# Turning half the heads' probabilities in 32x32 blocks on VectorE and multiplying them in 32-row tiles on TensorE

## The chip, the cores and the metric

One core of a Trainium2 chip runs the whole kernel. The metric is device time in microseconds of one execution. TensorE (PE, with its weight loads as PEld), VectorE (DVE), ScalarE (ACT), GpSimd (POOL) and SyncE (SP, which issues most DMAs) each run their own queue in order.

## The reference

Sixteen heads (batch 2 x 8) of attention over 768 positions of 64 channels, with a mask: a query sees only keys whose 6 sign bits of a random projection are equal. Two layers of matrix products follow.

```python
q_bits = (np.einsum('bhsd,dk->bhsk', q, proj) > 0)      # k_bits alike; bucket = bits as a number
mask = q_bucket[:, :, :, None] == k_bucket[:, :, None, :]
scores = np.where(mask, scale * np.matmul(q, k.transpose(0, 1, 3, 2)), -1e9)
scores = scores - np.max(scores, axis=-1, keepdims=True)
attn = np.exp(scores)
attn = attn / (np.sum(attn, axis=-1, keepdims=True) + 1e-09)
x = np.matmul(attn, v)                                  # to (1536 tokens, 512)
h = np.maximum(np.maximum(x @ w1, x @ w2), x @ w3) @ w_out
h = h @ w_in                                            # 512 to 2048
g = np.where(h >= 1, h, np.where(h <= -1, 0.0, (h + 1) ** 2 / 4))
out = g @ w_out2
```

## The kernel before

**Attention, one tile.** A head has NK = 6 query tiles of 128 rows, so there are 96 tiles n = 6 h + t. A tile takes these steps. `t_qk` (L369) makes the scores of 128 queries against 768 keys with four matmuls into one of two score buffers `s_ps`; the mask is folded in by extra rows of the operands, and the scores carry a minus sign, so that the maximum is a minimum. `t_max` (L385) copies them to an SBUF tile `p` on VectorE and takes the row minimum at the same time. `t_exp` (L394) makes the exponential in place on ScalarE, with its row sums into `sums`. `t_tr` (L405) turns `p` with six TensorE transposes of 128x128, three into each of two PSUM banks (of three: the two `t_ps` and `pj_ps`). `t_out` (L413) copies each bank into `pt`, on ScalarE or VectorE, whichever the planner finds free first.

**Three tiles make a group.** `g_pv` (L422) multiplies a group of 384 queries: six f32 matmuls with V as the stationary operand (128 keys x 64 channels) and `pt` as the moving one, three key blocks summed on rows 0 to 63 of `u_ps` and the other three on rows 64 to 127. `g_copy` (L443) takes the result to SBUF, `g_fold` (L454) brings the two row halves together by DMA, and GpSimd adds them, multiplies by the reciprocal row sums and splits the result into a high and a low part `x_hl` for the matrix products.

**Preparation.** For each head, K and Q come by one DMA, GpSimd scales and splits them in high and low parts, four DMAs move rows, and TensorE projects the bits (`bits_mm`, L351), which VectorE compares (`bits_rows`, L357).

**Order.** Each step is a task with an engine, a cost, a due time, what it comes after, and the buffers it takes and leaves. A planner (`Work.run`, L76) plays the tasks through with these costs when the program is built and writes each engine's queue in the order that comes out. TensorE's order is written out by hand (L696 to L704): transposes of tile n, scores of tile n + 3, and a group's V product after the next group's first tile. Heads follow one another.

**After attention** come the matrix products (`mlp`), in three-term f32 splits. Their weights come in slices: each is loaded, split on ScalarE, VectorE and GpSimd (`w_steps`, L193) and kept in one of WEARLY early buffers, or, once the attention pools are given up, one of WBUFS - WEARLY later ones (L220). The first steps use tokens of batch 0 and slices 0 to 2.

Of the kernel before, what the change touches and what calls it, by code (L numbers as in the profile page):

```python
# [19 lines left out]
NK = S // 128  # L20
CH = 256
# [91 lines left out]
def lsh_attention_moe_kernel(  # L113
# [3 lines left out]
    v: bass.AP,  # L117
    pj: bass.AP,
# [52 lines left out]
    WEARLY, WBUFS = 5, 7  # L171
# [88 lines left out]
    def attention(mlp_steps):  # L260
        with ExitStack() as ax, ExitStack() as sx:
            raw_p = ax.enter_context(tc.tile_pool(name="raw", bufs=2))
            prep_p = ax.enter_context(tc.tile_pool(name="prep", bufs=3))
            v_p = ax.enter_context(tc.tile_pool(name="v", bufs=2))
            p_p = ax.enter_context(tc.tile_pool(name="p", bufs=3))
            pt_p = ax.enter_context(tc.tile_pool(name="pt", bufs=3))
# [3 lines left out]
            t_ps = [ps_s.tile([128, 512], F32, name=f"t_ps{i}") for i in range(2)] + [pj_ps]  # L270
            NH, NT_ = B * H, B * H * NK
            head, pair, tl, grp = {}, {}, {}, {}

            def warm_up(count, i):
                for _ in range(count):
                    nc.tensor.matmul(out=t_ps[i][:, 0:CH], lhsT=warm[:, 0:128], rhs=warm, start=True, stop=True)


            def load_head(h, parts=1):
# [6 lines left out]
                head[h] = dict(r=r)  # L286

            def load_v(h):
                vr = v_p.tile([128, NK, D], F32, tag="vr", name="vr", bufs=3)
                nc.sync.dma_start(out=vr, in_=v[h])  # L290
                head[h]["vr"] = vr
# [72 lines left out]
            def bits_both(h, bank):  # L364
                for half in range(2):
                    bits_mm(h, half, t_ps[bank.at], 64 * half)


            def t_qk(n):  # L369
# [3 lines left out]
                for half in range(2):  # L373
                    ks = slice(half * HALF, (half + 1) * HALF)
                    o = s_ps[n % 2][:, half, 0:HALF]
# [9 lines left out]
            def t_max(n):  # L385
                nm = sm_p.tile([128, 1], F32, tag="nm", name="nm", bufs=4)
                p = p_p.tile([128, S], F32, tag="p", name="p")
                nc.vector.tensor_scalar(  # L388
                    out=p.rearrange("p (a k) -> p a k", a=2), in0=s_ps[n % 2][:, :, 0:HALF], scalar1=MASKED, scalar2=MASKED,
                    op0=ALU.min, op1=ALU.min, accum_out=nm,  # L390
                )
                tl[n] = dict(nm=nm, p=p)

            def t_exp(n):  # L394
                h, t = divmod(n, NK)
                if n % (2 * NK) == 0:
                    pair[h // 2] = dict(sums=nm_p.tile([128, 64], F32, tag="sums", name="sums")[:, 0:2 * NK])
# [4 lines left out]
                    accum_out=pair[h // 2]["sums"][:, c:c + 1],  # L402
                )

            def t_tr(n, half, bank):  # L405
                for j in range(3):
                    kt = 3 * half + j
                    nc.tensor.transpose(  # L408
                        out=t_ps[bank.at][:, j * 128:(j + 1) * 128],
# [3 lines left out]
            def t_out(n, half, bank, copy):  # L413
                g, r = divmod(n, 3)
                if g not in grp:
                    grp[g] = pt_p.tile([128, NK, HALF], F32, tag="pt", name="pt")
                copy(  # L417
                    out=grp[g][:, 3 * half:3 * half + 3, r * 128:(r + 1) * 128],
                    in_=t_ps[bank.at][:, 0:HALF].rearrange("p (j q) -> p j q", j=3),
                )  # L420

# [8 lines left out]

            def block(g, bits, bank):
                if bits:
                    bits_both(bits, bank)
                    for half in range(2):
                        bits_rows(bits, half, t_ps[bank.at], 64 * half)
                    work.at["DVE"] = work.at.get("DVE", 0.0) + 1.38
                g_pv(g, 0, 3)
# [16 lines left out]
            def g_fold(g):  # L454
                pr, cs = g_cut(g)
                if g % 4 == 0:
                    pr["uc"] = nm_p.tile([128, S], F32, tag="uc", name="uc", bufs=1)
# [22 lines left out]
            def pair_rows(p_, bank=pj_ps):  # L480
                nc.tensor.transpose(out=bank[0:2 * NK, 0:128], in_=pair[p_]["sums"], identity=ident)

            def pair_copy(p_, bank=pj_ps):
                rt = nm_p.tile([2 * NK, 128], F32, tag="rt", name="rt", bufs=1)
                nc.scalar.copy(out=rt, in_=bank[0:2 * NK, 0:128])
# [64 lines left out]
            raw_s = {x: Slots(1) for x in ("rb", "rt", "u_ps", "uc")}  # L550
            raw_s["prep"] = Slots(3)
            raw_s["pt"], raw_s["t"] = Slots(3), Slots(3)
            raw_s |= {x: Slots(2) for x in ("r", "uo", "s", "xr", "sums", "u", "d")}
            raw_s["p"] = Slots(3)
            raw_s["vr"] = Slots(3)
# [4 lines left out]
            def task(eng, cost, due, fn, *args, **kw):  # L560
                return work.add(eng, cost, lambda: fn(*args), due, **kw)
# [6 lines left out]
            def head_tasks(h):  # L568
                due = NK * h - 11
# [16 lines left out]
                if h == 1:  # L586
                    bp = place("t", 1)
                    mm = task("PE", 0.66, due + 1, bits_both, h, bp, after=[hi], takes=[bp], leaves=[rp])
                    order["bits"] = [mm]
                    rows = [  # L590
                        task("DVE", 0.69, due + 1, lambda half=half: bits_rows(h, half, t_ps[bp.at], 64 * half), after=[mm])
                        for half in range(2)
# [8 lines left out]
            def v_tasks(h):  # L601
                due = NK * h - 2
                vr = place("vr", 2)
                v_place[h] = vr
                if h > 0:
                    vready[h] = task("SP", 0.35, due, load_v, h, takes=[vr], lag=3.0)
# [4 lines left out]
            sums_p, u_p, uc_p, exps, adds, pt_p_ = {}, {}, {}, {}, {}, {}  # L611

            def tile_tasks(n):
                h, t = divmod(n, NK)
                g, r = divmod(n, 3)
                sp, pp = place("s", 1), place("p", 2)
                tb = [place("t", 1) for i in range(2)]
                if n % (2 * NK) == 0:
# [333 lines left out]
```

## Time and profile before

| | |
|---|---|
| median of 3 runs | 694.81 us (693.83 to 695.39) |
| profiled execution, its own time | 694.73 us |
| its span, first to last instruction | 693.0 us |
| TensorE busy | 683.4 us (99%) |
| VectorE busy | 491.3 us (71%) |
| ScalarE busy | 344.9 us (50%) |
| GpSimd busy | 273.0 us (39%) |

The profiled execution is one run; its time lies close to the median, and 1.7 us of it lie outside the span. A busy time is the union of an engine's instructions. Matmuls are pipelined, so a new one starts before the one ahead is recorded as ended, and a busy TensorE says less than the pace at which its instructions follow one another. In the span three stages can be told apart: the start to 14.80 us, attention to 231.65, and the matrix products.

### The profile page before, as it was taken

Reading aid. Unit: us, or ns where it says so; the run is one execution under the profiler, and the core shown is the slowest. Engines: PE = TensorE matmul, PEld = TensorE weight load, DVE = VectorE, ACT = ScalarE, POOL = GpSimd, SP = SyncE. Lnnn points to the kernel's source line nnn. Section 1 sums busy time; section 2 is a strip of 40 time slices with the busy share of each in tenths; the row PEclk is TensorE's granted clock in tenths of the full one; section 3 lists DMA queues with packets and bytes.
Section 4 is the critical chain, followed back from the end, with each engine's and each line's share of the span. In section 5 each row is a group of like instructions: output and inputs, shape, how many; then the busy total and the mean of one; then the engine's idle time right before and its main releaser. Section 6 shows DMA issues by size and latency. Waiting matters only on the chain.

```text
span 693.0 us, 9878 instructions
## 1 busy us (share of the span) xinstructions
PE 683.4 (99%) x3516; PEld 541.3 (78%) x3516; DVE 491.3 (71%) x758; ACT 344.9 (50%) x669; POOL 273.0 (39%) x248
## 2 busy tenths in 40 slices
PE   7999999999999999999999999999999999999998
PEld 4777777677767688888888888888888888888886
DVE  6778787787776586775444356765888888888844
ACT  3777677777768333332322233665454444554430
POOL 4234564654730334443232112534434434434430
PEclk9999999999999999999999999999999999999999
DMA  5656576475541322221112022121111112211104
GB/s 157 131 135 142 138 195 159 115 177 140 141 101 39 107 92 91 92 92 53 47 45 69 31 70 88 56 78 45 61 61 62 61 61 66 85 62 61 31 0 183
DMA packets 26281, 62.76 MB, mean 91 GB/s; under 512 B 3940, under 2 KB 10692, under 8 KB 26232
## 3 DMA queue, kind: packets, MB, share of 16 engines
q1 hardware_dynamic: 26200, 62.12, 31.6%
q8 instruction: 28, 0.46, 0.3%
q14 instruction: 21, 0.17, 0.1%
q0 software_dynamic: 32, 0.00, 0.0%
HBM read 42.04 MB, written 3.19 MB: 65 GB/s over the span
## 4 chain that ended last, share of the span: by engine, by line
PE 94%; DVE 4%; ACT 1%; issue 1%; DMA 0%; DVEq 0%; ACTq 0%
PE b L746 47%; PE b L873 19%; PE u_ps L426 8%; PE t_ps L408 6%; PE s_ps L378 4%; PE s_ps L381 4%; PE pj_ps L408 3%; DVE p L388 1%; PE t_ps L352 1%; PE pj_ps L352 1%; DVE q L359 1%; DVE pt L417 1%; DVE lo L312 0%; ACT p L400 0%; DMA r<-in_kq 0%
## 5 line engine op out<-in xcount | busy, mean ns | idle before, releaser
L746 PE MATMUL b<-x_hl,w 128*128 128x512 f32 (+1 forms) x900 | 202.0, 381 | 0.0
L746 PEld LDWEIGHTS b<-x_hl,w 128*128 128x128 f32 x900 | 163.9, 188 | 33.1 <-issue 0.6
L773 POOL TENSOR_TENSOR g<-r,g 128x512 fp32r<-128x512 f32 x48 | 62.5, 1303 | 121.3 <-ACT g L772 121.3
L873 PE MATMUL b<-w,g 128*128 128x512 f32 (+1 forms) x438 | 105.9, 386 | 0.0
L388 DVE TENSOR_SCALAR_CACHE_REDUCE p<-s_ps 128x768 f32<-128x768 f32 x96 | 91.6, 956 | 15.8 <-PE s_ps L381 13.8
L400 ACT ACTIVATE p<-p,nm 128x768 f32<-128x768 f32 x96 | 90.1, 939 | 17.9 <-DVE p L388 16.9
L873 PEld LDWEIGHTS b<-w,g 128*128 128x128 f32 x438 | 81.5, 188 | 16.7
L230 POOL TENSOR_TENSOR w<-wg,w 128x512 fp32r<-128x512 f32 (+1 forms) x42 | 59.4, 1414 | 84.4 <-ACT w L224 68.6
L203 DVE SCALAR_TENSOR_TENSOR wg<-wg,wr 128x512 f32<-128x512 f32 (+1 forms) x58 | 66.1, 1140 | 35.6 <-ACT wg L201 34.8
L746 PE MATMUL b<-x_hl,wx 128*128 128x512 f32 x360 | 84.0, 389 | 0.0
L224 ACT CAST w<-wg 128x512 fp32r<-128x512 f32 (+1 forms) x42 | 25.5, 606 | 117.2 <-DVE wg L216 117.2
L746 PEld LDWEIGHTS b<-x_hl,wx 128*128 128x128 f32 x360 | 67.6, 188 | 14.0
L378 PE MATMUL s_ps<-lo,q 128*128 128x384 f32 x192 | 73.2, 381 | 3.5 <-DVE p L388 2.4
L426 PE MATMUL u_ps<-pt,vr 128*64 128x384 f32 x384 | 69.0, 491 | 0.2 <-DVE pt L417 0.2
L381 PE MATMUL s_ps<-hi,q 76*128 76x384 f32 x192 | 65.5, 341 | 0.7 <-DVE hi L343 0.7
L853 DVE SCALAR_TENSOR_TENSOR r<-r,b 128x512 f32<-128x512 f32 x48 | 33.0, 687 | 44.2 <-ACT r L852 44.2
L880 DVE TENSOR_TENSOR acc<-b,acc 128x512 f32<-128x512 f32 (+1 forms) x85 | 56.3, 675 | 7.7 <-PE b L873 7.6
L408 PE MATMUL t_ps<-ident,p 128*128 128x128 f32 x384 | 58.7, 275 | 0.3
L208 DVE TENSOR_SCALAR wg<-wg 128x512 int32<-128x512 int32 (+1 forms) x58 | 53.8, 927 | 2.8
L851 ACT ACTIVATE r<-b,half_sb 128x512 f32<-128x512 f32 x48 | 33.0, 687 | 41.3 <-PE b L746 41.3
L408 PEld LDWEIGHTS t_ps<-ident,p 128*128 128x128 f32 x384 | 45.8, 141 | 9.1 <-issue 4.8
L216 DVE SCALAR_TENSOR_TENSOR wg<-wr,wg 128x512 int32<-128x512 int32 (+1 forms) x58 | 51.7, 892 | 1.0
(87 smaller groups left out, 898.1 us busy)
## 6 DMA issues: line engine op xcount, KB each, us to landing
wr<-in_w SPq DMA_DIRECT2D x48, 512.0 KB
r<-in_kq SPq DMA_DIRECT2D x15, 384.0 KB
q<-hi SPq DMA_DIRECT2D x15, 384.0 KB
vr<-in_v SPq DMA_DIRECT2D x16, 192.0 KB
rb<-d SPq DMA_DIRECT2D x16, 192.0 KB
wr<-in_w SPq DMA_DIRECT2D x8, 384.0 KB
q<-lo SPq DMA_DIRECT2D x15, 192.0 KB
lo<-hi SPq DMA_DIRECT2D x15, 192.0 KB
```

Source lines behind the costliest of these rows:

```text
L203: nc.vector.scalar_tensor_tensor(out=f32(g), in0=f32(g), scalar=TINY_SQ, in1=f32(high), op0=ALU.is_ge, op1=ALU.mult)
L230: nc.gpsimd.tensor_tensor(out=w[:, 1, 0:cols], in0=f32(g2), in1=f32(w[:, 0, 0:cols]), op=ALU.subtract)
L378: nc.tensor.matmul(out=o, lhsT=hd["qa"][:, qs], rhs=hd["lo"][:, ks], start=True, stop=False)
L381: nc.tensor.matmul(out=o, lhsT=hd["qb"][0:76, qs], rhs=hd["hi"][0:76, ks], start=False, stop=True)
L388: nc.vector.tensor_scalar(out=p.rearrange("p (a k) -> p a k", a=2), in0=s_ps[n % 2][:, :, 0:HALF], scalar1=MASKED, scalar2=MASKED, op0=ALU ...
L400: nc.scalar.activation(out=p, in_=p, func=ACTF.Exp, scale=-1.0, bias=tl[n]["nm"], accum_out=pair[h // 2]["sums"][:, c:c + 1],)
L408: nc.tensor.transpose(out=t_ps[bank.at][:, j * 128:(j + 1) * 128], in_=tl[n]["p"][:, kt * 128:(kt + 1) * 128], identity=ident,)
L426: nc.tensor.matmul(out=u_ps[rows, 0:HALF], lhsT=vr[:, kt, :], rhs=grp[g][:, kt, :], start=(i == 0), stop=(i == 2),)
L746: nc.tensor.matmul(out=outp, lhsT=w_[a], rhs=x_[b_], start=(i == 0 and jj == 0), stop=(i == n - 1 and jj == 2),)
L773: nc.gpsimd.tensor_tensor(out=dst[:, 1, cs], in0=src, in1=f32(dst[:, 0, cs]), op=ALU.subtract)
L873: nc.tensor.matmul(out=pb[:, cs], lhsT=gs[f][:, a, tsl], rhs=wt[:, b_, cs], start=(n == 0), stop=(n == len(terms) - 1),)
L880: nc.vector.tensor_tensor(out=acc[:, t, cs], in0=pb[:, cs], in1=acc[:, t, cs], op=ALU.add)
```

## The change

Heads 2, 4, ... 14 (seven heads, 42 tiles) are turned in another way. VectorE transposes the tile `p` in 32x32 blocks into `dt` (`t_turn`), in place of six TensorE transposes and two copies out of PSUM. In `dt` the keys of a block lie on 32 partitions, and which 32 tells which quarter of the 128 queries they belong to. `block4` multiplies a whole head at once: for each of 24 key blocks and each of the four row quarters one matmul of 32 rows x 64 columns, 192 queries wide, the quarters into four banks (`u_ps`, both of `t_ps`, `pj_ps`), even key blocks on rows 0 to 63 and odd ones on 64 to 127. V has to lie on all four row quarters, so it is loaded four times over (`v4`). Three copies (`copy4`) and one DMA (`fold4`) take the result out. The other heads keep their way, but both banks of a tile are copied at once, on ScalarE, while the heads alternate.

The tiles of the turned heads alternate with those of the odd heads (`SEQ`), behind head 0 and the first four tiles of head 1. TensorE's order is written out as strings of steps by place in that sequence: q scores, t transposes, v and w the first and the second part of a V product, b bits, r row sums. `SHIFT` moves the due times of the kinds of tasks. The early weight buffers go from five to three, the prepared heads from three to four, `p` from three to four, `pt` from three to two, `vr` from three to one beside one `v4`. One small constant is loaded by ScalarE's queue, and the scratch for GpSimd's DMAs is smaller.

```diff
-    WEARLY, WBUFS = 5, 7
+    WEARLY, WBUFS = 3, 7
...
-            t_ps = [ps_s.tile([128, 512], F32, name=f"t_ps{i}") for i in range(2)] + [pj_ps]
+            dt = pt_p.tile([128, NK + 2, NB, 32], F32, name="dt", bufs=1)
+            t_ps = ps_s.tile([128, 2, 512], F32, name="t_ps")
...
+            TURNED = range(2, B * H, 2)
+            LEAD = 4
+            first, second = range(NK), [NK * h + t for h in range(1, B * H, 2) for t in range(NK)]
+            DT_AT = {h: 2 * (h // 2 % 2) for h in TURNED}
+            TILES = lambda h: [(t - DT_AT[h]) % NK for t in range(NK)]
+            turned = [NK * h + t for h in TURNED for t in TILES(h)]
+            SEQ = [*first, *second[:LEAD], *(n for ab in zip(turned, second[LEAD:]) for n in ab), *second[LEAD + len(turned):]]
+            SLOT = {n: m for m, n in enumerate(SEQ)}
...
+            def load_v4(h, i):
+                if i == 0:
+                    head.setdefault(h, {})["vr"] = v_p.tile([128, NB, D], F32, tag="v4", name="v4", bufs=1)
+                ks = slice(i * NB // 3, (i + 1) * NB // 3)
+                nc.sync.dma_start(out=head[h]["vr"][:, ks], in_=v4[h, :, ks])
...
+            def t_turn(n):
+                h, t = divmod(n, NK)
+                nc.vector.transpose(out=dt[:, DT_AT[h] + t], in_=tl[n]["p"].rearrange("p (b k) -> p b k", k=32))
+
+            def quarter(q):
+                return (u_ps, t_ps[:, 0], t_ps[:, 1], pj_ps)[q]
+
+            def block4(h, lo, hi):
+                vr, at = head[h]["vr"], slice(DT_AT[h], DT_AT[h] + NK)
+                for kb in range(lo, hi):
+                    cols = UP if kb % 2 == 0 else DOWN
+                    for q in range(4):
+                        rows = slice(32 * q, 32 * q + 32)
+                        nc.tensor.matmul(
+                            out=quarter(q)[cols, 0:NK * 32].rearrange("p (t k) -> p t k", t=NK), lhsT=vr[rows, kb, :], rhs=dt[rows, at, kb],
+                            start=kb < 2, stop=kb >= NB - 2,
+                        )
+
+            def copy4(h, q, count, copy):
+                pr = pair[h // 2]
+                if "u" not in pr:
+                    pr["u"] = nm_p.tile([128, S], F32, tag="u", name="u")
+                to = pr["u"].rearrange("p (t g k) -> p g t k", t=NK, g=4)
+                if count == 1:
+                    copy(out=to[:, q], in_=quarter(q)[:, 0:NK * 32].rearrange("p (t k) -> p t k", t=NK))
+                else:
+                    copy(out=to[:, q:q + 2], in_=t_ps[:, :, 0:NK * 32].rearrange("p a (t k) -> p a t k", t=NK))
+
+            def fold4(h):
+                pr = pair[h // 2]
+                pr["uc"] = nm_p.tile([128, S], F32, tag="uc", name="uc", bufs=2)
+                nc.sync.dma_start(out=pr["uc"][UP], in_=pr["u"][DOWN])
...
+            T_AT, P_AT = 2, 1
+            START = {h: min(SLOT[NK * h + t] for t in range(NK)) for h in range(NH)}
+            raw_s = {x: Slots(1) for x in ("rb", "rt", "u_ps", "t", "b", "v4", "vr")}
+            raw_s |= {x: Slots(2) for x in ("r", "uo", "s", "xr", "sums", "u", "uc", "d", "pt")}
+            raw_s["prep"], raw_s["p"], raw_s["dt"] = Slots(4), Slots(4), Slots(8)
+
+            SHIFT = {prep_hi_scaled: 6.0, t_exp: 42.5, t_out: 2.0, g_copy: 17.5, copy4: -82.0, pair_copy: -20.5, w_tick: 60.0, prep_lo_scaled: -3.0, bits_rows: 4.5, t_max: -12.5, t_turn: 8.0, pair_recip: 20.0}
...
+                    pt_p_[n] = place("dt", 1)
+                    tu = task("DVE", 0.96, m - 1, t_turn, n, after=[ex] + outs.get(h, [])[-1:], takes=[pt_p_[n]], leaves=[pp])
+                    outs.setdefault(h, []).append(tu)
+                    return
...
+                    cp = task(*ways[0][:2], m - 4, t_out, n, hs, ways[0][2], after=[tr], takes=[pt_p_[g]] if r == 0 and (half == 0 or not alone) else [], leaves=[tb])
+                    if alone:
+                        work.also(*ways[1][:2], lambda a=(n, hs, ways[1][2]): t_out(*a), cp)
+                    outs.setdefault(("g", g), []).append(cp)
...
+            def turned_tasks(h):
+                m = max(SLOT[NK * h + t] for t in range(NK))
+                banks = [place("u_ps", 1), place("t", 1), place("b", 1)]
+                blk = None
+                for i in range(2):
+                    blk = task(
+                        "PE", 1.955, m + T_AT + 0.5, block4, h, 12 * i, 12 * i + 12, after=[blk] if i else outs[h] + [vready[h]],
+                        takes=[] if i else banks, leaves=[pt_p_[n] for n in turned if n // NK == h] + [v_place[h]] if i else [],
+                    )
+                    order[f"pv{2 * h}.{i}"] = [blk]
+                takes = own(u_p, "u", h // 2, 2)
+                cps = []
+                for q, count, place_, act, dve in ((1, 2, banks[1], 0.5, 0.56), (0, 1, banks[0], 0.35, 0.36), (3, 1, banks[2], 0.35, 0.36)):
+                    cps.append(task("ACT", act, m - 2, copy4, h, q, count, nc.scalar.copy, after=[blk] + cps[:1], takes=[] if cps else takes, leaves=[place_]))
+                adds[2 * h] = adds[2 * h + 1] = task("SP", 0.5, m + 4, fold4, h, after=cps, takes=own(uc_p, "uc", h // 2, 2), lag=4.5)
...
+            first_part = (
+                "q0 q1 B q2 t0 q3 q4 t1 t2 q5 b5 t3 v2 w2 t4 q6 q11 b8 t5 q7 q8 t6 v5 w5 q9 t7 q10 q12 t8 "
+                "q13 q14 t9 v8 q15 t11 q18 w8 q23 q16 t13 b13 q17 t15 v13 w13 q19 r13 t17 q20 b19 q21 t19 "
+            )
+            period = (
+                "q22 q24 v19 w19 t21 q25 q26 v20 w20 q27 t23 q30 q28 t25 b25 q29 q35 t27 v25 w25 q31 r25 "
+                "t29 q32 b31 q33 t31 "
+            )
+            last_part = (
+                "q82 q84 v79 w79 t81 q85 q86 v80 w80 q87 t83 q90 q88 t85 q94 q89 t87 v85 w85 q91 t94 q95 "
+                "r85 t89 q92 q93 t91 t95 v91 w91 t93 v92 w92 "
+            )
+            steps = first_part.split()
...
-        nc.gpsimd.dma_start(out=pc_sb, in_=pc)
+        nc.scalar.dma_start(out=pc_sb, in_=pc)
...
+    v4 = np.tile(v.reshape(B * H, NB, 32, D).transpose(0, 2, 1, 3), (1, 4, 1, 1))
```

## Rows read from the trace of the kernel before

**Rows 1.** The page, engines: busy us (share of the span) x instructions.

```profile
PE 683.4 (99%) x3516; PEld 541.3 (78%) x3516; DVE 491.3 (71%) x758; ACT 344.9 (50%) x669; POOL 273.0 (39%) x248
```

**Rows 2.** Busy times by stage: stretch, length, each engine's busy time, clock, DMA share, GB/s.

```profile
14.80:231.65 216.85, 214.01 (x1400) 153.97 (x1401) 163.78 (x326) 157.14 (x345) 98.79 (x110) 1.00 0.55 134
231.65:254.70 23.05, 23.05 (x137) 20.30 (x136) 17.01 (x27) 7.94 (x15) 6.27 (x5) 1.00 0.33 109
```

**Rows 3.** Chain of waits, 100 to 112 us: start, time on the chain, what.

```profile
102.72 2.09 PE u_ps L426 x12
104.81 0.48 PE pj_ps L408 x3
...
105.61 0.18 PE s_ps L378
...
107.70 0.66 PE t_ps L408 x6
...
109.07 0.80 PE pj_ps L352 x4
109.87 1.94 PE u_ps L426 x12
```

**Rows 4.** Chain of waits over the attention stage, two of its longest pieces.

```profile
22.62 2.09 PE u_ps L426 x12
...
49.28 2.09 PE u_ps L426 x12
```

**Rows 5.** Groups by line and shape, attention stage: count, busy us, mean ns, idle before.

```profile
L388 DVE TENSOR_SCALAR_CACHE_REDUCE p<-s_ps 128x768 f32<-128x768 f32 x95 | 90.6, 956 | 15.8 <-PE s_ps L381 13.8 <-PE t_ps L408 0.6 <-ACT p L400 0.6
...
L400 ACT ACTIVATE p<-p,nm 128x768 f32<-128x768 f32 x96 | 90.1, 939 | 17.9 <-DVE p L388 16.9
...
L426 PE MATMUL u_ps<-pt,vr 128*64 128x384 f32 x384 | 69.0, 491 | 0.2 <-DVE pt L417 0.2
...
L417 ACT COPY pt<-t_ps 128x384 f32<-128x384 f32 x71 | 33.0, 478 | 12.8 <-PE t_ps L408 12.7
...
L417 DVE COPY pt<-t_ps 128x384 f32<-128x384 f32 x57 | 31.3, 553 | 19.8 <-PE t_ps L408 16.0 <-ACT uo L451 1.8 <-ACT u L448 1.6
...
L417 ACT COPY pt<-pj_ps 128x384 f32<-128x384 f32 x39 | 18.7, 479 | 6.1 <-PE pj_ps L408 6.0
...
L417 DVE COPY pt<-pj_ps 128x384 f32<-128x384 f32 x25 | 13.8, 552 | 3.7 <-PE pj_ps L408 3.6
```

**Rows 6.** Timeline of TensorE: f32 projections of one half, and of both halves.

```profile
5.44 0.86 PE L352 MATMUL pj_ps<-r,pj_sc 128*64 128x384 f32 x2
...
109.00 0.87 PE L352 MATMUL pj_ps<-r,pj_raw 128*64 128x384 f32 x4
```

**Rows 7.** Timeline of TensorE's weight loads at the start of a V block.

```profile
102.65 0.20 PEld L426 LDWEIGHTS u_ps<-pt,vr 128*64 128x64 f32 x4 [0.26 <-issue]
...
103.03 0.14 PEld L426 LDWEIGHTS u_ps<-pt,vr 128*64 128x64 f32 x2 [0.18 <-issue]
```

**Rows 8.** Timeline of VectorE in the preparation of head 0.

```profile
6.64 0.36 DVE L343 CAST q<-lo 64x384 fp32r<-64x384 f32 x1
```

**Rows 9.** The page's costliest groups: the weight split on VectorE.

```profile
L203 DVE SCALAR_TENSOR_TENSOR wg<-wg,wr 128x512 f32<-128x512 f32 (+1 forms) x58 | 66.1, 1140 | 35.6 <-ACT wg L201 34.8
```

**Rows 10.** Timeline of VectorE, two minima back to back.

```profile
16.18 0.96 DVE L388 TENSOR_SCALAR_CACHE_REDUCE p<-s_ps 128x768 f32<-128x768 f32 x1
...
17.06 0.95 DVE L388 TENSOR_SCALAR_CACHE_REDUCE p<-s_ps 128x768 f32<-128x768 f32 x1
```

**Rows 11.** What TensorE waited for in the attention stage: total, times, longest.

```profile
PE s_ps L378 <- DVE p L388: 2.4, 3, 1.4
```

**Rows 12.** DMA queues, attention stage: packets, MB, share of 16 engines.

```profile
q1 hardware_dynamic: 14950, 28.73, 54.1%
```

**Rows 13.** Timeline of GpSimd behind the attention stage: weight slices 3 and 4.

```profile
244.86 1.36 POOL L230 TENSOR_TENSOR w<-wg,w 128x512 fp32r<-128x512 f32 x1 [4.33 <-ACT w L224]
...
251.73 1.74 POOL L230 TENSOR_TENSOR w<-wg,w 128x512 fp32r<-128x512 f32 x1
```

More of the change, by code (lines that the diff above doesn't have):

```diff
@@ L586, in head_tasks @@
                 if h == 1:
-                    bp = place("t", 1)
-                    mm = task("PE", 0.66, due + 1, bits_both, h, bp, after=[hi], takes=[bp], leaves=[rp])
+                    bp = place("b", 1)
+                    mm = task("PE", 0.644, due + 1, bits_both, h, after=[hi], takes=[bp], leaves=[rp])
                     order["bits"] = [mm]
                     rows = [
-                        task("DVE", 0.69, due + 1, lambda half=half: bits_rows(h, half, t_ps[bp.at], 64 * half), after=[mm])
-                        for half in range(2)
+                        task("DVE", 0.69, due + 1, bits_rows, h, half, pj_ps, 64 * half, after=[mm]) for half in range(2)
                     ]
@@ L615, in tile_tasks @@
                 g, r = divmod(n, 3)
-                sp, pp = place("s", 1), place("p", 2)
-                tb = [place("t", 1) for i in range(2)]
-                if n % (2 * NK) == 0:
-                    sums_p[h // 2] = place("sums", 1)
+                turned = h in TURNED
+                sp, pp = place("s", 1), place("p", 1 if turned else 2)
+                takes = own(sums_p, "sums", h // 2, 1)
+                qk = task("PE", 0.72, m, t_qk, n, sp, after=ready[h], takes=[sp], leaves=[h_place[h]])
@@ L628, in tile_tasks @@
+                tb = place("t", 2 if alone else 1)
+                tr = None
                 for half in range(2):
[L629 removed]
+                    tr = task("PE", 0.288, m - 4, t_tr, n, half, after=[ex, tr], takes=[] if half else [tb], leaves=[pp], lag=0.1)
                     order[f"tr{n}"] = order.get(f"tr{n}", []) + [tr]
[L631 removed]
@@ L696, in attention @@
-            names = ["qk0", "qk1", "bits", "qk2"]
-            for g in range(NT_ // 3):
-                for n in range(3 * g, 3 * g + 3):
-                    names += [f"tr{n}", f"qk{n + 3}"]
-                    if n == 3 * g and g:
-                        names += [f"pv{g - 1}"] + ([f"rows{g // 4 - 1}"] if g % 4 == 2 else [])
-            line = [t for x in names for t in order.get(x, ())]
-            for a, b_ in zip(line, line[1:]):
-                b_["after"].append(a)
-            low = exps[30]
+            starts = sorted(range(1, NH), key=START.get)
@@ new lines, in attention @@
+            blocks = sorted((g for g in range(NT_ // 3 - 1) if g // 2 not in TURNED), key=lambda g: SLOT[3 * g + 2])
+            BITS = dict(zip(blocks[1:], starts[1:]))
+            assert len(BITS) == len(starts) - 1
+            made = 0
+            for m, n in enumerate(SEQ):
+                h, t = divmod(n, NK)
+                if m == 0:
+                    v_tasks(0)
+                while made < len(starts) and (made < 3 or START[starts[made]] <= m + 18):
+                    head_tasks(starts[made])
+                    v_tasks(starts[made])
+                    made += 1
+                tile_tasks(n)
+                if h in TURNED:
+                    if TILES(h)[-1] == t:
+                        turned_tasks(h)
+                elif n % 3 == 2:
+                    if n < NT_ - 1:
+                        group_tasks(n // 3)
```

218 lines of the change are left out of this document (117 added, 101 removed).

## The prediction

> **What bounds the kernel now.** I read the page's engine shares first, then the busy times by stage, then the chain of waits inside the attention stage, then the groups of instructions of that stage. TensorE is busy for 99% of the span [rows 1], so the question is which of its work goes away and whether it stays fed. The change touches the attention stage alone, 14.80 to 231.65 us, 216.85 us long; TensorE is busy in 214.01 us of it at a granted clock of 1.00, VectorE in 163.78 (76%) and ScalarE in 157.14 (72%) [rows 2]. Busy times of pipelined matmuls overstate their cost, so I take paces from the chain [rows 3]. It runs through TensorE without a gap: a score matmul takes 0.18 us, so the four of a tile some 0.71, its six transposes 0.66, a group of three tiles times V 1.94 to 2.09, the bit projections of a head 0.80. Transposes right after a V block take 0.48 for three where the others take 0.33, so a change of tile shape costs about 0.15. Two heads take 26.66 us (22.62 to 49.28, the same place in the pattern four groups later) [rows 4].
>
> **What is removed on TensorE.** Seven heads of six tiles are turned: 42 x 6 = 252 transposes at 0.66 / 6 = 0.11 us [rows 3], 27.7 us.
>
> **What replaces the multiplication.** Now a head is two groups of six f32 matmuls of 384 columns; the trace holds 384 records for 32 x 6 matmuls, so each is two records [rows 5]. The pair on output rows 0 to 63 and 64 to 127 runs side by side: one f32 matmul of 384 columns alone (two records) spans 0.86 us, two on the two column halves (four records) 0.87 [rows 6]. Three pairs take 1.94 us, 0.647 a pair [rows 3]; a head costs 3.88. After, a head is 24 key blocks x 4 row quarters = 96 matmuls of 192 columns, 192 records and as many weight loads. No row shows a 32-row matmul, so this is the disputed price. From below: if all eight tiles (four row quarters, two column halves) run together, a round of eight takes half of 0.647, and 12 rounds take 3.88, no change. From above: if only the column halves run together, 48 pairs x 0.323 = 15.5 us, 11.6 more per head and 81 more in all. Between them lies the issue: the first four loads of a V block are over after 0.20 us where two take 0.14 [rows 7], so two more cost 0.06, 0.03 each with no overlap; if loads and matmuls together were issued no faster, 384 x 0.03 = 11.5 us a head. I take the lower end, since the nearest row, two tiles of one array, shows that tiles overlap fully, loads included, and keep the upper ones as rivals.
>
> [...]
>
> The block also takes all of u_ps, t_ps (both banks) and pj_ps at once, so TensorE starts it only when each has been copied out, and the transposes behind it wait for the block's first copy. In the written order two score steps (2 x 0.71) stand ahead of each block and one (0.71) behind, against a copy of 0.48 and a hand-over. If ScalarE has just begun an exponential the copy is late by up to its 0.939 [rows 5]; seven heads, 6.6 us at most. Fewer changes of shape give back 0.15 per head, 1 us, which I leave in that margin.
>
> **VectorE.** It loses its copies of transposed tiles, 82 x 0.553 = 45.3 us [rows 5], and keeps perhaps 12 of them, 6.6, for the ten tiles ahead of the alternation and the two after it. It gains 42 block transposes of 128x768. No row shows one. From below: an f32 copy between SBUF tiles of 64x384 took 0.36 [rows 8], twice that is 0.72. From above: the two-input operation on 128x512 took a mean of 1.14 [rows 9], which at 768 columns is 1.71. I take 0.956, the row of the same size and type (the running minimum), so 40.2 us. Sum: 163.8 - 45.3 + 6.6 + 40.2 = 165.3 us. Back to back the minimum starts every 0.88 us (16.18, 17.06), less than its 0.956 and its accumulator read [rows 10], so there is more room than the sum says.
>
> **ScalarE.** It loses 110 copies x 0.478 = 52.6 us [rows 5] and gets 42 copies of both halves, at most two of 0.478 each, 40.2, and 12 single ones, 5.7. Per turned head three copies replace two, at most 0.48 more, 3.4. Sum 157.1 - 52.6 + 49.3 = 153.8 us. The projections, minima, exponentials, sums and the preparation on GpSimd are the same in number.
>
> **TensorE's sum.** 216.85 - 27.7 = 189.1 us. VectorE would be busy in 87% of that, ScalarE in 81%, so TensorE stays the bound, but with less slack: there are two score buffers and four tiles p. Its waits on VectorE's minima are now 2.4 us in three places [rows 11]. After, VectorE has to be done with a minimum before the score step two later. Between the blocks the written order has stretches such as q27 t23 q30 q28 t25 b25 q29 q35 t27, five score steps in 5 x 0.71 + 3 x 0.66 + 0.80 = 6.3 us; five minima alone take 4.4 of it, so turns of 0.956 are left for the blocks of 3.9 us, in which no score is made. I allow 6 us for the added waits, about one late copy or minimum of an exponential's length in each of the seven alternating stretches; bounds 0 and 14 (two of them).
>
> **DMA.** A turned head's V comes four times over: 768 KB in three pieces for 192 KB, 7 x 576 KB = 4.1 MB more on 28.73 MB, now 54.1% of the engines' time in the stage [rows 12]. In a stage of 195 us that is 54.1 x 32.9 / 28.7 x 217 / 195 = 69%. SP issues three loads and one fold for one load and two folds, one more per head. With one buffer, V of the next turned head is fetched after the block before, and has the rest of the pattern, 26.7 - 4.0 (six tiles' transposes) - 3.9 = 18.8 us; 768 KB at 28.73 MB in 217 us (132 GB/s) take 6 us. I cost it at nothing under that cover; if it went, each late load would stop TensorE by what it is late, 6 us at most. Ready K and Q for the alternating pair come by the same queue; one more prep buffer covers that. The constant moved from GpSimd's queue to ScalarE's, the added buffer of uc, the sums' own place and the smaller scratch are not on the chain: nothing.
>
> **Weights of the next stage.** Three early buffers for five: slice 3 was finished on GpSimd at 246.2 and slice 4 at 253.5 [rows 13], inside the 23.05 us in which TensorE works on slices 0 to 2, to 254.70 [rows 2]. Now slice 3 begins behind the sixth early step, half-way, at 231.65 + 11.5 = 243.2; at the 7.3 us that lie between two slices there [rows 13] it is ready by 250.5, 4 us early, and each next one 7.3 us later for 7.7 us of use. Nothing; without that cover, TensorE waits as long as it is late.
>
> **Sum.** The profiled execution took 694.73 us for a span of 693.0, as the median does (694.81): 694.7 - 27.7 + 6 = 673.0.
>
> **Rivals.** (1) *The tiles overlap in part.* Against: the column pair loses nothing [rows 6]. For: six times as many instructions per multiply, loads of 0.03 and more. A block of 5 to 6 us is 1.2 to 2.1 more for each head, 8 to 15 us: 681 to 688. [...]
> (2) *VectorE becomes the bound.* A turn at 1.71 makes it 165.3 + 42 x 0.75 = 197 busy against 189; counted at the minimum's pace of 0.88 it is some 15 less, 182. Then little slack is left and waits eat 12 to 18 us instead of 6: 679 to 685. Against: a stage at equal loads still drops the copies.
> (3) *The block is bound by issue or runs row by row, and the time is longer.* Place: the 384 instructions of a block. TensorE has 21.7 us to lose, 3.1 per head, so it turns when a block takes over 7.0 us, 18 ns an instruction. At 0.03 it is 11.5: 673 + 7 x 7.6 = 726; row by row 754. For: the loads' spacing [rows 7]. Against: that spacing was seen where the array itself was occupied.
>
> **How the numbers follow.** Forecast 0.60 (667 to 681), rival 1 0.14, rival 2 0.09, rival 3 0.17. Of rival 3, 0.03 comes out within 0.2% (1.4 us, what a measurement here can tell from no change) and 0.14 slower. Faster is 0.60 + 0.14 + 0.09 = 0.83. The range takes in the forecast and rivals 1 and 2 and stops where rival 3 begins, 664 to 694; its low end is 667 less the 1 us of shape changes and 2 of today's waits. What it leaves out is rival 3's slower part and a few hundredths below.
>
> **What would show it.** The attention stage ends at 208 to 213 instead of 231.65; 324 transposes remain; a block of 192 matmul records spans 3.9 us; the turn's mean is near 0.96; TensorE idles under 10 us in the stage; the rest, from the first MLP matmul, is unchanged at 461 us. The prediction is wrong if a block takes over 5 us, if the turn takes over 1.3, or if waits on s_ps or t_ps come to more than 14 us.

## The result, and the profile after

The changed kernel takes 675.67 us (median of 4 runs, 675.43 to 676.23) against 694.44 us (693.83 to 695.39) in the same comparison: a ratio of 0.973, with a 95% interval of 0.9713 to 0.9747. That is 18.8 us less. The forecast was 673.0, with 664 to 694 as its range. The profiled execution took 676.23 us for a span of 674.4.

The page, engines (busy us, share, instructions), to be held against [rows 1]:

```profile
PE 662.3 (98%) x4440; PEld 530.3 (79%) x4440; DVE 492.3 (73%) x725; ACT 337.3 (50%) x625; POOL 273.4 (41%) x247
```

Busy times by stage, with the columns of [rows 2]. The first MLP matmul now starts at 213.06:

```profile
14.80:213.06 198.26, 190.60 (x2312) 140.95 (x2310) 161.87 (x292) 147.22 (x297) 101.24 (x111) 1.00 0.65 166
213.06:236.10 23.04, 23.04 (x136) 20.14 (x135) 14.91 (x24) 6.85 (x13) 3.87 (x3) 1.00 0.30 94
```

The whole gain lies in the attention stage: it ends 18.6 us earlier (231.65 to 213.06), and from there to the end of the span pass 461.3 us, as before (693.0 less 231.65). The granted clock stays at 1.00. TensorE idles for 7.7 us of the stage (198.26 less 190.60), where it was 2.8.

Groups of the stage by line and shape, as in [rows 5] (count, busy us, mean ns, idle before):

```profile
L405 DVE TENSOR_SCALAR_CACHE_REDUCE p<-s_ps 128x768 f32<-128x768 f32 x94 | 87.8, 950 | 11.2 <-PE s_ps L398 8.8 <-PE t_ps L428 0.7 <-issue 0.3
...
L445 DVE STREAM_TRANSPOSE dt<-p 128x768 f32<-128x768 f32 x42 | 40.2, 969 | 9.7 <-PE pj_ps L456 9.3
...
L438 ACT COPY pt<-t_ps 128x768 f32<-128x768 f32 x42 | 33.4, 796 | 12.4 <-PE t_ps L428 12.2
L456 PE MATMUL t_ps<-dt,v 32*64 32x192 f32 x672 | 30.5, 324 | 1.1 <-issue 0.7 <-ACT pt L438 0.4
```

The minimum takes what it took, 0.950 us, and the turn 0.969, 40.2 in all. The copy of both banks takes 0.796, less than two single ones of 0.478 [rows 5]. The next rows are TensorE's timeline at the start of the block of head 4:

```profile
85.43 0.37 PE L456 MATMUL u_ps<-dt,v 32*64 32x192 f32 x1
85.44 0.38 PE L456 MATMUL t_ps<-dt,v 32*64 32x192 f32 x2
85.45 0.37 PE L456 MATMUL pj_ps<-dt,v 32*64 32x192 f32 x1
85.46 0.37 PE L456 MATMUL u_ps<-dt,v 32*64 32x192 f32 x1
85.47 0.38 PE L456 MATMUL t_ps<-dt,v 32*64 32x192 f32 x2
85.48 0.37 PE L456 MATMUL pj_ps<-dt,v 32*64 32x192 f32 x1
85.65 0.32 PE L456 MATMUL u_ps<-dt,v 32*64 32x192 f32 x1
...
85.81 0.32 PE L456 MATMUL u_ps<-dt,v 32*64 32x192 f32 x1
```

Eight records, one for each row quarter and column half, start within 0.05 us, and the next eight 0.16 to 0.22 us later. In the steady part such a round takes 0.162 us, and the 24 rounds of a block 3.9 us. A matmul is two records (192 for the 96 of a block), so eight whole matmuls take two rounds, 0.324 us. That is half of the 0.647 us that a pair of matmuls took before [rows 3], with half as many columns: eight tiles side by side cost no more than two. No loss is to be seen.

The chain of waits for one period of the alternation, from block to block, as in [rows 3, 4] (start, time on the chain, what):

```profile
61.28 0.30 PE u_ps L456
...
64.38 0.31 issue
...
66.20 0.37 PE s_ps L395
...
69.87 0.80 PE pj_ps L369 x4
70.67 0.37 PE s_ps L395
...
72.94 2.08 PE u_ps L480 x12
75.02 0.37 PE s_ps L395
...
77.41 0.80 PE pj_ps L369 x4
78.20 0.37 PE s_ps L395
...
81.19 2.09 PE u_ps L480 x12
83.27 0.81 PE t_ps L428 x6
...
85.50 0.30 PE u_ps L456
...
89.59 0.37 PE s_ps L395
```

Two heads take 24.22 us here, and 23.9 as a mean of the six periods from 61.21 to 204.62, where they took 26.66 [rows 4] and 22.7 (26.66 less 3.96) would have been all of the transposes' gain. Three things are to be seen. A block takes 4.09 us from 85.50 to 89.59, but 4.92 from 61.28 to 66.20, with a hole at 64.38 that the trace puts down to "issue". Behind each of the four narrow steps (32 rows or 64 columns) that a score follows, the first score matmul takes 0.37 instead of 0.18; behind the V product at 81.19, the transposes take 0.81 instead of 0.66. And there are five such visits to narrow shapes in two heads, where there were four: the bits used to stand right ahead of a V product.

What TensorE waited for (total, times, longest), as in [rows 11]:

```profile
PE s_ps L395 <- DVE p L405: 2.7, 2, 1.8
PE t_ps L428 <- ACT pt L438: 2.0, 3, 0.9
...
PE u_ps L480 <- ACT u L467: 0.9, 1, 0.9
...
PE t_ps L456 <- ACT pt L438: 0.4, 1, 0.4
PE s_ps L398 <- DMA hi<-q: 0.3, 1, 0.3
```

Of these waits only 1.4 us fall into the six periods from 61.2 to 204.6 (1.1 for copies, 0.3 for the DMA); the rest lie ahead of them or behind. The DMA queue of [rows 12] now moves this in the stage:

```profile
q1 hardware_dynamic: 16239, 32.61, 63.8%
```

### The profile page after: what moved, and what is told of

Read it like the earlier page. It is cut to its first block, busy times and chain, and to the rows that moved or that the text cites. A ratio compares the mean times of both kernels' runs of the same rounds, so it can differ in the third digit from the quotient of the medians.

```text
span 674.4 us, 11567 instructions
## 1 busy us (share of the span) xinstructions
PE 662.3 (98%) x4440; PEld 530.3 (79%) x4440; DVE 492.3 (73%) x725; ACT 337.3 (50%) x625; POOL 273.4 (41%) x247
## 4 chain that ended last, share of the span: by engine, by line
PE 94%; DVE 2%; DMA 2%; ACT 1%; issue 1%; SPq 0%; DVEq 0%; ACTq 0%
PE b L867 49%; PE b L994 19%; PE s_ps L395 5%; PE u_ps L480 5%; PE t_ps L428 5%; PE s_ps L398 4%; PE u_ps L456 3%; PE pj_ps L369 2%; PE t_ps L456 1%; DVE p L405 1%; DVE lo L329 1%; DMA r<-in_kq 1%; DMA rb<-d 0%; ACT pt L438 0%; PE pj_ps L456 0%
## 5 line engine op out<-in xcount | busy, mean ns | idle before, releaser
L867 PE MATMUL b<-x_hl,wx 128*128 128x512 f32 x684 | 159.6, 389 | 0.0
L867 PEld LDWEIGHTS b<-x_hl,wx 128*128 128x128 f32 x684 | 128.4, 188 | 26.7
L867 PE MATMUL b<-x_hl,w 128*128 128x512 f32 (+1 forms) x576 | 126.8, 376 | 0.0
L867 PEld LDWEIGHTS b<-x_hl,w 128*128 128x128 f32 x576 | 103.1, 188 | 20.7 <-issue 0.6
L420 ACT ACTIVATE p<-p,nm 128x768 f32<-128x768 f32 x96 | 89.7, 935 | 12.3 <-DVE p L405 11.6
L232 POOL TENSOR_TENSOR wx<-wg,wx 128x512 fp32r<-128x512 f32 (+1 forms) x32 | 45.6, 1425 | 65.4 <-ACT wx L226 48.5
L994 PE MATMUL b<-wx,g 128*128 128x512 f32 x288 | 72.1, 389 | 0.0
L994 PE MATMUL b<-w,g 128*128 128x512 f32 (+1 forms) x294 | 71.3, 385 | 0.0
L994 PEld LDWEIGHTS b<-w,g 128*128 128x128 f32 x294 | 54.5, 188 | 11.1
L994 PEld LDWEIGHTS b<-wx,g 128*128 128x128 f32 x288 | 54.0, 188 | 11.2
L232 POOL TENSOR_TENSOR w<-wg,w 128x512 fp32r<-128x512 f32 (+1 forms) x26 | 36.0, 1384 | 58.3 <-ACT w L226 48.1
```

What stands on the lines that cost most here:

```text
L232: nc.gpsimd.tensor_tensor(out=w[:, 1, 0:cols], in0=f32(g2), in1=f32(w[:, 0, 0:cols]), op=ALU.subtract)
L420: nc.scalar.activation(out=p, in_=p, func=ACTF.Exp, scale=-1.0, bias=tl[n]["nm"], accum_out=sums_of(h // 2)[:, c:c + 1],)
L867: nc.tensor.matmul(out=outp, lhsT=w_[a], rhs=x_[b_], start=(i == 0 and jj == 0), stop=(i == n - 1 and jj == 2),)
L994: nc.tensor.matmul(out=pb[:, cs], lhsT=gs[f][:, a, tsl], rhs=wt[:, b_, cs], start=(n == 0), stop=(n == len(terms) - 1),)
```

## The experiments

Each run is set against the changed kernel's 675.67 us; a ratio is to the kernel before on the same chip.

**Rows in turn.** Is the side by side of the row quarters what makes the block cheap?

```diff
-                for kb in range(lo, hi):
-                    cols = UP if kb % 2 == 0 else DOWN
-                    for q in range(4):
+                for q in range(4):
+                    for kb in range(lo, hi):
+                        cols = UP if kb % 2 == 0 else DOWN
```

> The 48 matmuls of each half of a turned head's block are issued quarter by quarter instead of in turn over the four row quarters; the work is the same. If the block is cheap because eight 32x64 tiles run together, only the two column halves are left side by side: 48 pairs x 0.323 = 15.5 us a block for 3.9, seven heads, 81 us more: about 757 us. If the order doesn't matter (tiles wait for each other anyway, or start out of order), about 676.

It took 782.12 us in one run, more than either theory gave. Busy times of three stretches of this run, the first two around the first block, the third over all seven:

```profile
60.00:69.78 9.78, 9.78 (x162) 8.50 (x163) 2.90 (x7) 2.61 (x6) 7.46 (x9) 1.00 0.38 83
69.79:80.02 10.23, 10.23 (x58) 8.77 (x54) 3.57 (x6) 3.62 (x8) 0.00 (x0) 0.50 0.32 90
...
60.00:320.00 260.00, 258.69 (x2057) 197.06 (x2057) 122.37 (x221) 114.43 (x228) 81.44 (x91) 0.76 0.37 96
```

The first block begins at 60.26. Its first half takes 5.76 us at a granted clock of 1.00, which makes an estimated 11.5 us for a block instead of 3.9, so the order decides the price. At 69.79, still inside this block, the granted clock falls from 1.00 to 0.50, though TensorE had been busy for all of the 9.78 us before; the block takes 13.6 us in all. Over the seven blocks the granted clock is 0.76 on average, and the later ones take 18 to 20 us. Of the 106 us more, an estimated 7 x (11.5 - 3.9) = 53 are the order's own; the rest, by difference, goes with the clock.

**Two rows.** The same, with two quarters at a time.

```diff
-                for kb in range(lo, hi):
+                for q0, kb, q in ((q0, kb, q) for q0 in (0, 2) for kb in range(lo, hi) for q in (q0, q0 + 1)):
```

> The matmuls of each half block are issued for two row quarters first and then for the other two: four tiles run together instead of eight. [...]

It took 687.97 us in one run, 12.3 more. A block takes 6.1 us (first round at 86.17, last at 92.16). TensorE's timeline, one round of four records and the start of the next:

```profile
86.39 0.32 PE L456 MATMUL u_ps<-dt,v 32*64 32x192 f32 x1
86.39 0.32 PE L456 MATMUL t_ps<-dt,v 32*64 32x192 f32 x1
86.40 0.32 PE L456 MATMUL u_ps<-dt,v 32*64 32x192 f32 x1
86.41 0.32 PE L456 MATMUL t_ps<-dt,v 32*64 32x192 f32 x1
86.55 0.32 PE L456 MATMUL u_ps<-dt,v 32*64 32x192 f32 x1
```

A round costs the same 0.16 (86.39 to 86.55) with half the tiles in it, which would make 7.8 us a block and 27 us more for seven. Only 6.1 are seen. That the runs of the two pairs of quarters overlap at their ends would fit, as it would for the quarters of the run above (an estimated 11.5 for 15.5), but these rows do not show a place where they meet. From its start to the next step each of the first six blocks takes 6.24 us, 2.15 more than the 4.09 of an undisturbed block of the changed kernel. For seven that makes 15 us; but none of them has a hole like the one at 64.38, and the changed kernel's three holes add 2.8. The clock stays at 1.00. So the side by side of the quarters is shown, with its price: an estimated 11.5 us for one at a time, 6.1 for two, 3.9 for four.

**Short turn, double turn.** How far is VectorE from being the bound?

```diff
-                nc.vector.transpose(out=dt[:, DT_AT[h] + t], in_=tl[n]["p"].rearrange("p (b k) -> p b k", k=32))
+                nc.vector.transpose(out=dt[:, DT_AT[h] + t, 0:1], in_=tl[n]["p"].rearrange("p (b k) -> p b k", k=32)[:, 0:1])
...
-                            out=quarter(q)[cols, 0:NK * 32].rearrange("p (t k) -> p t k", t=NK), lhsT=vr[rows, kb, :], rhs=dt[rows, at, kb],
+                            out=quarter(q)[cols, 0:NK * 32].rearrange("p (t k) -> p t k", t=NK), lhsT=vr[rows, kb, :], rhs=dt[rows, at, 0],
```

> Each turn on VectorE takes 32 of the 768 columns, and the block reads that one key block 24 times; the other key blocks are left out of the result. The queues' order is the same. VectorE loses 42 x (0.969 - some 0.2) = 32 us. If TensorE's own work sets the end, only waits on VectorE go: 1 to 4 us less, 672 to 675. If VectorE is as much the bound as TensorE, 10 us or more less, under 666.

It took 675.87 us, 0.9724 (0.9699 to 0.9748): nothing, although a turn takes 0.203 us instead of 0.969 and VectorE is busy for 28 us less in the span (463.9 for 492.3). Even the 1 to 4 us of the first expectation did not come.

```diff
+                for _ in range(2):
                     nc.vector.transpose(out=dt[:, DT_AT[h] + t], in_=tl[n]["p"].rearrange("p (b k) -> p b k", k=32))
```

> Each turn is made twice, 42 x 0.97 = 41 us more on VectorE, which is busy for 162 of the 198 us of the stage. If TensorE sets the end and VectorE has slack, the slack of some 36 us takes most of it, but in bursts: 5 to 15 us more, 681 to 691. If VectorE is the bound, nearly all of it: 35 to 41 us more, 711 to 717.

It took 703.36 us, 1.0126 (1.0098 to 1.0154): 27.7 of the 41 us added come through, which lies between the two expectations. The granted clock was 0.98 in the stage, which is an estimated 4 us at most (2% of TensorE's 199 busy), so 13 to 17 us were slack. What TensorE waited for then:

```profile
PE s_ps L395 <- DVE p L405: 19.2, 22, 2.1
```

Together: VectorE's work is wholly hidden as it stands, and some 13 us more of it would be.

**Fewer transposes.** Is TensorE still the bound, to the full price of what it loses?

```diff
-                for j in range(3):
+                for j in range(1 if NK + LEAD <= SLOT[n] < NT_ - 2 else 3):
```

> The tiles of the odd heads that alternate with the turned ones make two of their six TensorE transposes; what the others would have written is left out, so the products of those heads are wrong in two thirds of the keys. TensorE loses 42 x 4 x 0.11 = 18.5 us, no other engine loses anything. If TensorE sets the end: 12 to 18 us less, 658 to 664. If VectorE or ScalarE are as much the bound: under 5 less, over 671.

It took 666.48 us, 0.9602 (0.9573 to 0.9631): 9.2 of 18.5 us, again between the two expectations. A step of two transposes takes 0.22 us as expected, but waits come up that were not there:

```profile
PE s_ps L395 <- DVE p L405: 5.0, 14, 0.9
```

**Both less.** Is it VectorE that keeps the other half? Both edits at once.

> The edits of short_turn and fewer_transposes together: 32 of 768 columns turned, two of six transposes made for the odd heads' alternating tiles; the rest of both is left out of the result. Alone they gave 0 and 9 us of the 32 and 18.5 us that they take off VectorE and TensorE. If VectorE's load is what kept the missing transposes from giving more, both together give 14 to 18 us: 658 to 662. If it is the order, ScalarE or the transfers, it stays at 665 to 668.

It took 664.41 us, 0.9574 (0.9558 to 0.959), 2 us below the one edit alone, with intervals that overlap. So VectorE holds back little of the rest or nothing. TensorE's waits are spread, in a profiled execution that took 669.29 us with a granted clock of 0.96 in the stage:

```profile
PE s_ps L398 <- DMA hi<-q: 2.7, 2, 2.3
PE s_ps L395 <- DVE p L405: 2.6, 2, 1.7
```

What else keeps the other 7 us is open.

**Bits at V, early bits.** Fewer visits to narrow shapes: the bit projections right ahead of a V product, as before the change, instead of between score steps; first moved later, then earlier. The repeated part of the order stands here for the others, first the later ones:

```diff
-                "q22 q24 v19 w19 t21 q25 q26 v20 w20 q27 t23 q30 q28 t25 b25 q29 q35 t27 v25 w25 q31 r25 "
-                "t29 q32 b31 q33 t31 "
+                "q22 q24 b19 v19 w19 t21 q25 q26 v20 w20 q27 t23 q30 q28 t25 q29 q35 t27 b25 v25 w25 q31 r25 "
+                "t29 q32 q33 t31 "
```

> In TensorE's written order each bit projection stands directly ahead of a group's V product, as in the kernel before, instead of between score steps. Both have 64-column tiles, so two changes of tile shape at some 0.15 us go for each of 13 projections: 2 to 4 us less than with the change alone, 671.5 to 674. If the projections then come too late for the heads that need them, TensorE waits for their rows: 676 or more.

It took 683.92 us, 0.9848 (0.9819 to 0.9876), 8 more: the expectation missed, the rival held. What TensorE waited for:

```profile
PE s_ps L395 <- DVE p L405: 4.6, 7, 1.5
PE s_ps L398 <- DMA hi<-q: 3.5, 5, 1.1
```

```diff
-                "q22 q24 v19 w19 t21 q25 q26 v20 w20 q27 t23 q30 q28 t25 b25 q29 q35 t27 v25 w25 q31 r25 "
-                "t29 q32 b31 q33 t31 "
+                "q22 q24 v19 w19 t21 q25 q26 v20 w20 q27 t23 q30 q28 t25 b25 q29 q35 t27 b31 v25 w25 q31 r25 "
+                "t29 q32 q33 t31 "
```

> Six of the bit projections are put directly ahead of the V product that comes before their old place, some 4 us earlier: six visits to 64-column tiles fewer, and the rows that the next head waits for come earlier, not later. By the visits' price of 0.25: 1.5 us less, 673.5 to 675. If the projected head isn't split yet at that time, TensorE waits for GpSimd: 676 or more.

It took 681.83 us, 0.982 (0.9803 to 0.9837), 6 more: missed again. Here the data are early, not late, and waits come all the same:

```profile
PE s_ps L395 <- DVE p L405: 3.1, 8, 0.9
PE u_ps L480 <- ACT pt L438: 2.3, 5, 0.5
```

In both, score steps that had a projection between them follow each other directly, and TensorE then waits for minima in seven or eight places instead of two. That a projection there is partly paid for by a wait that it fills fits this. The rows shown account for 5.1 of the 8 us (4.6 + 3.5 less the 3.0 of the profile after) and 2.7 of the 6; the rest was not isolated. The planner also writes the other engines' queues anew for each order.

**Split visits.** The price of a visit itself: the two parts of 15 V products parted by a score or transpose step, same work, 15 visits more.

```diff
-                "q22 q24 v19 w19 t21 q25 q26 v20 w20 q27 t23 q30 q28 t25 b25 q29 q35 t27 v25 w25 q31 r25 "
+                "q22 q24 v19 t21 w19 q25 q26 v20 w20 q27 t23 q30 q28 t25 b25 q29 q35 t27 v25 q31 w25 r25 "
```

> In TensorE's written order one score or transpose step is put between the two parts of 15 V products, so TensorE goes to 64-column tiles and back 15 times more; work and waits for data are the same. If it is such visits that gave back a part of the gain (scores right behind one take 0.90 us for 0.72, and a start 0.1 more than a step elsewhere), 15 x 0.25 = 3.8 us more than the change alone: 678.5 to 680.5. If the longer scores behind them were waits for VectorE or ScalarE, the visits cost nothing by themselves: 675 to 677.

It took 679.21 us, 0.9785 (0.9771 to 0.9798): 3.5 more, 0.24 a visit, as expected. In its chain of waits, one V product in two visits (0.80 and 1.44 for 2.08):

```profile
73.49 0.80 PE u_ps L480 x4
74.28 0.38 PE s_ps L395
...
75.19 1.44 PE u_ps L480 x8
```

The 0.24 is a net figure. Two such places, each from the start of the V product to a later step that stands alike in both orders, take 0.26 and 0.33 us longer than in the changed kernel, an estimated 4.4 us for 15. But the holes inside the blocks, to which the next run turns, add only 1.1 us in this run's profile and 2.8 in the changed kernel's.

**Shifted code.** The holes inside blocks stand in heads 2, 6 and 10 and not in 4, 8 and 12. Is it the place of the tiles in `dt`, which alternates the same way, or the place of the code? 64 small matmuls, 128 instructions, are added ahead of one early tile.

```diff
+                    if n == SEQ[16] and half == 0:
+                        for _ in range(64):
+                            nc.tensor.matmul(out=o[:, 0:32], lhsT=warm[:, 0:128], rhs=warm[:, 0:32], start=True, stop=True)
```

> 64 small matmuls with their loads, 128 instructions, are put ahead of the scores of one early tile; their results are overwritten. They cost some 4 us once. In the profile of the change, four of the seven blocks (heads 2, 6, 10, 14) have a gap of 0.6 to 0.9 us that no wait explains, some 2.8 us into the block. If it is the fetch of TensorE's instructions, which depends on where the block lies in the code, the gaps move to the other blocks (heads 4, 8, 12) or to other places in them. If it is the place of those heads' tiles in dt, or their loads, the gaps stay in heads 2, 6, 10 and 14.

It took 676.3 us in one run. TensorE's timeline of the changed kernel in head 2:

```profile
64.05 0.32 PE L456 MATMUL u_ps<-dt,v 32*64 32x192 f32 x1
64.69 0.38 PE L456 MATMUL t_ps<-dt,v 32*64 32x192 f32 x2 [0.31 <-issue]
```

and of this kernel in head 4, where the changed kernel has no hole:

```profile
88.20 0.32 PE L459 MATMUL u_ps<-dt,v 32*64 32x192 f32 x1
89.77 0.38 PE L459 MATMUL t_ps<-dt,v 32*64 32x192 f32 x2 [1.24 <-issue]
```

The holes moved to heads 4, 8 and 12, and 2, 6 and 10 have none: they go with the place in TensorE's instruction stream, not with the data. The expectation counts head 14 too, but its gap is another: it lies 0.2 us into the block, has the same length in both runs, and the trace names a wait for a copy (the 0.4 us above).

The packets of the DMA queue that the trace names q8 instruction (16 KB each) say more. In the changed kernel one starts 1.0 to 1.7 us after the start of a block with a hole (at 62.23, 110.79 and 159.38), and 2.5 to 3.0 us after the start of those in heads 4, 8 and 12 (at 88.24, 136.51 and 185.08). The first three end at 63.13, 112.18 and 160.69, and the first matmul behind the hole starts at 64.69, 113.62 and 162.03, 1.3 to 1.6 us later. The changed kernel and ten of these runs have 31 blocks with such a hole. In them that packet ends anywhere from 1.5 to 3.9 us into the block, and each time the first matmul behind the hole starts 1.2 to 1.6 us after that end; the latest packet has the longest hole (2.0 us, in V extra, 1.6 of them idle). In two rows, where the same 384 instructions are spread over 6.2 us, no block has a hole. So the holes go with these packets in time; what links the two, no run shows.

**V twice, V extra.** How thick is the cover over the loads of V? First each piece loaded twice into the same tile, then the second time to a scratch in DRAM that nobody waits for.

```diff
-                nc.sync.dma_start(out=head[h]["vr"][:, ks], in_=v4[h, :, ks])
+                for _ in range(2):
+                    nc.sync.dma_start(out=head[h]["vr"][:, ks], in_=v4[h, :, ks])
```

> The fourfold V of a turned head is loaded twice, 7 x 768 KB = 5.5 MB more and three issues on SP for each head. If the loads lie under the work as the prediction costed them: within 1 us of the change alone, 675 to 677. If the queue of transfers is near its limit (its share is 0.64 to 0.81 of the stage): 5 us or more, over 681.

It took 713.34 us, 1.027 (1.0244 to 1.0295), 38 more, as the second expectation has it. The waits of SP's queue and of TensorE in it:

```profile
SPq L309 <- DMA v<-in_v: 66.4, 21, 4.5
```

```profile
PE s_ps L399 <- DMA hi<-q: 18.5, 8, 3.8
```

Each second load stands in SP's queue until the first has landed, and the transfers of K and Q stand behind it.

```diff
                 nc.sync.dma_start(out=head[h]["vr"][:, ks], in_=v4[h, :, ks])
+                vx = dr_p.tile([128, NB // 3, D], F32, tag="vx", name="vx", bufs=6)
+                nc.sync.dma_start(out=vx, in_=v4[h, :, ks])
```

> Behind each piece of a turned head's V the same piece is loaded once more, but into a scratch of its own in DRAM, so that no transfer waits for another: 5.5 MB and 21 issues on SP more, without the wait that the second load into the same tile had. If loading V twice cost 38 us because SP's queue stood still behind those waits (62.6 us in 20 waits), this costs 0 to 3 us: 675 to 679. If the transfers themselves are near their limit, it costs most of it again: over 695.

It took 681.65 us, 0.9813 (0.9793 to 0.9833), 6 more, between the two expectations.

```profile
PE s_ps L400 <- DMA hi<-q: 5.4, 3, 3.3
```

So the same bytes read once more cost 6, nearly all of it in waits for the moved rows of K and Q, and none for V. Where the queue stands still as well, these waits grow to 18.5, and the granted clock in that stage is 0.93, an estimated 14 us at most (7% of TensorE's 206 busy); together they are most of the 38. The change's own extra V shows only as the 0.3 us that TensorE waits for `hi<-q` in the profile after.

## Why the prediction was right, point by point

**TensorE was the bound and stayed it.** The step "252 transposes at 0.11, 27.7 us" came true: transposes take 4.1 us of a period where they took 8.5. The stage gained 18.6 of these, so 9.1 were lost again, for which the forecast had 6 (bounds 0 to 14). Fewer transposes shows that what TensorE loses still counts, but only by half from here on.

**The block at 3.88.** Right, at the lower end of a wide bracket (3.88 to 15.5): 24 rounds of 0.162. The reason given for the lower end, that column tiles had overlapped without loss, carried over to row quarters, and the two runs in which only the order differs (an estimated 11.5 us and 6.1 for 3.9) show that it is this overlap. In the stage an undisturbed block costs 4.1, the 0.2 being the way in and out. With the three holes, and two waits for copies around the last block, the seven take 4.8 on average and two of them over 5, which the prediction named as a sign of being wrong; it is not rival 1's loss, since the rounds keep their 0.162. Rival 1 falls: no run shows the 5 to 6 us that it gives a block of four quarters in turn; an undisturbed one took 4.09 to the next step. In rows in turn, with one row quarter alone (start times from 62.32 us on), a round takes 0.162 us as well, its loads included, so what that order costs is fewer tiles at a time. Rival 3 falls too: the issue of 8 records and their loads fits into 0.162 us.

**VectorE.** The turn at 0.956 measured 0.969, VectorE's sum of 165.3 measured 161.9. Rival 2 falls by short turn. ScalarE's 153.8 measured 147.2, since one copy of 768 columns (0.796) costs less than two of 384.

**The 6 us of added waits: inside the bounds, wrong in kind.** This step put them on late copies and minima. Those waits are 2.7 us in two places for minima (2.4 in three before [rows 11]) and 3.3 in five for copies (0.2 before), some 3.4 us added. The 9.1 us are instead mainly in the alternation: a period takes 23.9 for 22.7, 1.2 more, 7.2 for the six; the other 1.9 lie ahead of them and behind, where the last block takes 6.0 to the next step instead of 4.1. In the period shown above, five visits to narrow shapes instead of four take some 0.3 behind them (four score matmuls 0.19 too long and one set of transposes 0.15, against four times 0.15), V products and block 0.2 more (4.17 + 4.09 against 8.06), and the hole 0.83. Of the six periods three have such a hole (0.83, 0.89 and 1.07), 0.5 a period. With 0.2 of waits (1.4 us over six periods) that makes the 1.2. The prediction had no term for the holes nor for the way in and out of a block. That the total came within 2.7 us of the forecast owes something to luck, since the allowance for waits took them up. The sentence that fewer changes of shape would give back 1 us had the wrong sign: they became more, and split visits prices one at 0.24.

**Transfers at nothing.** It held (0.3 us of waits; the queue's share 63.8% where 69% was estimated), but the queue has less room than the cover of 18.8 us for V suggests: 5.5 MB more already cost 6, on K and Q, which the prediction took as covered by one more buffer.

**Weights of the next stage at nothing.** It held: the first 23.04 us after attention are TensorE's alone, as before, and the rest is 461.3.

**The signs named.** The stage's end of 213.06 is at the edge of 208 to 213, the idle 7.7 under 10, the turn and an undisturbed block as said.

## What to carry to other kernels

Where TensorE is busy for 99% and another engine has a quarter of its time free, try handing that engine a rearrangement: here 27.7 us of TensorE's work went, 18.6 were gained, and the new order took back a third. Count the visits to narrow tile shapes in a written order as work of their own (0.24 to 0.3 us each here), but try before moving them: here two ways of moving the bit projections, to have fewer visits, cost 8 and 6 us, which fits a step that is partly free because it fills a wait. When small tiles replace a full one, let consecutive matmuls go to different row quarters; here the same matmuls cost an estimated 11.5 us a block quarter by quarter and 3.9 in turn over the quarters.

## What was not expected of the hardware

The clock: with the row quarters in turn, the granted clock fell from 1.00 to 0.50 at 69.79 us, 9.5 us into the first block, and was 0.76 on average from 60 to 320 us, with TensorE 99% busy; with two quarters at a time it stayed at 1.00.

Holes of up to 2.0 us in dense runs of small matmuls (384 instructions in 4 us). In shifted code, with 128 instructions put ahead of them, they moved from heads 2, 6 and 10 to 4, 8 and 12; in the runs read, they end 1.2 to 1.6 us after a 16 KB packet of the queue q8 instruction.

Runs of matmuls on different row quarters took less than their rounds add up to: 6.1 us for 7.8 in two rows, and an estimated 11.5 for 15.5 in rows in turn.
